# Attention and two expert stages: setup pinned ahead, the written order kept to unit 23, one prefill piece and late scatters of empty rows in place of four pieces

## The chip, the cores and the metric

The kernel runs on one core of one Trainium2 chip. The metric is the device time of one launch in microseconds. The core has TensorE (PE, matmuls), VectorE (DVE), ScalarE (ACT), GpSimd (POOL) and SyncE (SP, which issues most of the DMAs); 16 DMA engines serve them.

## What is computed

A linear attention with a per-channel decay, then two mixture-of-experts layers with one expert for each token. All in float32.

```python
# attention: B, H, S, D = 4, 8, 768, 48
f = 1 / (1 + exp(-f_logit))
for t in range(S):
    state = f[:, :, t, :, None] * state + einsum('bhd,bhe->bhde', k[:, :, t], v[:, :, t])
    y[:, :, t] = einsum('bhd,bhde->bhe', q[:, :, t], state)
x = y as [3072 tokens, 384]
# MoE 1: 8 experts, 384 -> 1024 -> 384
logits = normalize(x) @ normalize(emb).T / tau; e = argmax(logits); gate = softmax(logits)[e]
x1 = gate * (relu(x @ w1[e]) @ w2[e])
# MoE 2: the same size, for tokens with x1 @ w_skip > 0 only; the others keep x1
e, gate from softmax(x1 @ w_gate)
out = x1 + gate * (relu(x1 @ u1[e]) @ u2[e])
```

## The kernel before

**Attention.** The work is cut in 24 units: unit u is the chunk u // 4 of 128 positions of the batch row u % 4, all eight heads. For each unit the kernel loads q, k and f in one tile (`qkf`, four buffers, `a_load`) and v, takes exp and a running product of the decays (`gexp`, `scan`, `lnexp`, `nrm`), scales k and q with it (`khat`, `qp`, `qhat`), forms the masked scores (`score`, `amask`), multiplies with V and the state (`av`, copied out by `ytc`), updates the state (`kv`, `sup`; not for the last chunk, units 20 to 23), and projects to rows and router logits (`xout`, `xrow`, `xlg`). The work of several units overlaps. Which step of which unit comes in which iteration i (from -1 to 24) is written out by hand in the string STEADY, and in a second string from iteration 20 on; "khat+2" means khat of unit i + 2. Iteration i holds the score of unit i + 1. `ch` calls `pin`, which chains an instruction behind the last pinned one on its engine, so that the scheduler keeps the written order; before, it does so only up to iteration 20. What isn't pinned, the scheduler places by itself.

**Routing.** When four units of a chunk are done, `a_route` finds for each token the expert and its slot in the table `tab1` (448 ranks of 8 experts, rank-major, rows of 396 words), in ten small steps that letters R and Q in the order release; four indirect DMAs of POOL (`tab<-rows`, line 666) scatter the 128 rows each, at the letters S and T. Rows of the table that no token fills have to hold empty rows: `prefill` writes them beforehand from the tile `pf`, 512 rows at a time, from rank R0 = 192 on, in four pieces after the iterations 0, 1, 3 and 4. `tab2`, the table of the second layer, gets its seven pieces in iterations 15 to 19 and in block 0 of the experts.

**Between the stages.** After iteration 18 `star(0)` picks the expert with the most tokens so far (the star), and `w_load` loads its weights on SP; SP has to read the expert's number first. In iterations from 21 on the letter W lets `w_split` split pieces of its w1 in a high (ACT) and a low part (DVE). After iteration 21 `fill` raises the star's count to at least 318, the second half of the weights is loaded, and `x_load` reads the first 318 rows of the star from the table.

**Experts.** `experts` runs over blocks: block 0 is rows 0 to 317 of the star, block 1 the rest of the star up to 446 (it has at most 128 rows and goes through `flip1`), blocks 2 to 8 the other seven experts in falling order of their counts, each with a capacity out of CAPS1; then the same for the second layer. Steps f = 0 to 7 are the eight slices of the first product. In block 0 the last route's steps and its four scatters come after f = 0, `order(0)` after f = 2 (it sorts the experts and sets a flag when a count is over its capacity), and `x_load` of block 1 at f = 3. In block 1, at f = 3, `x_load` and `w_load` of block 2 follow each other on SP.

The setup is in two functions, `setup0` before the first unit, and `setup` (index tiles, the triangular matrix `lst`) at iteration 1, neither of them pinned:

```python
                if i == 1:
                    self.setup(st)
```

## Time and profile before

| | us |
|---|---|
| median of 3 runs | 591.59 (588.57 to 593.02) |
| the profiled execution | 590.0 |
| its span, first to last instruction | 588.3 |

Engines by busy share of the span: PE 95%, DVE 66%, ACT 55%, POOL 40%; mean granted clock of PE 0.979 of full speed. The DMA engines moved 101 MB. Times in the profile count from the span's start. A line of the profile's timeline has the start, the length, the engine with the line of the code, the operation, output <- input, shape, how often, and in brackets how long the engine had been idle before and what released it. In-order engines run their queue as it stands: an operation that waits holds all that is behind it.

### The profile page before, as it was taken

The page shows a single profiled execution, that of the slowest core. Times are in us where ns is not written, and L with a number is a line of the kernel's source. Part 1 is how long each engine was busy: PE and PEld are TensorE (multiplying, and loading weights), DVE is VectorE, ACT ScalarE, POOL GpSimd, SP SyncE. Part 2 cuts the span into 40 slices and gives each one's busy share as a digit, 9 for nine tenths or more (in the row PEclk, how much of TensorE's full clock was granted, in tenths as well). Part 3 has the DMA queues.
Part 4 walks back from the last instruction along what each step waited for, and adds up shares of the span by engine and source line. Part 5 has one row for each costly group of instructions (what it writes and reads, how often), then busy time and mean ns, then how long its engine had stood idle before and what let it go on. Part 6 is the DMA issues. An engine that isn't in the chain of part 4 may idle for free.

```text
span 588.3 us, 12419 instructions
## 1 busy us (share of the span) xinstructions
PE 557.7 (95%) x4549; PEld 528.5 (90%) x4551; DVE 389.0 (66%) x1125; ACT 323.7 (55%) x813; POOL 233.3 (40%) x231
## 2 busy tenths in 40 slices
PE   8699999988899999999999999999899999999992
PEld 4598999876799999999999999999799999999991
DVE  6699999997556857674878678856276637565000
ACT  7587777744536755565665555545165545544220
POOL 5577898785202500505076507442320203122111
PEclk9799999988999999999999999999899999999997
DMA  8999999967296542617082708630737077574700
GB/s 220 240 263 240 192 201 237 222 193 223 77 286 212 120 181 59 245 32 267 14 266 35 286 9 268 178 130 12 218 111 250 28 261 231 185 222 147 275 21 19
DMA packets 60367, 101.14 MB, mean 172 GB/s; under 512 B 16953, under 2 KB 48205, under 8 KB 60298
## 3 DMA queue, kind: packets, MB, share of 16 engines
q1 hardware_dynamic: 42138, 87.28, 50.1%
q0 software_dynamic: 17600, 12.95, 8.3%
q8 instruction: 38, 0.62, 0.5%
q14 instruction: 31, 0.25, 0.2%
q10 hardware_dynamic: 560, 0.03, 0.1%
HBM read 78.49 MB, written 27.17 MB: 180 GB/s over the span
## 4 chain that ended last, share of the span: by engine, by line
PE 64%; DVE 12%; issue 8%; DMA 8%; ACT 3%; POOL 3%; SPq 0%; POOLq 0%; DVEq 0%; ACTq 0%
PE ph L811 23%; PE pyt L811 22%; DMA xg<-tab 3%; DMA qkf<-qkf 2%; PE pxt L801 2%; PE pa L554 2%; PE py L576 2%; DVE at L561 2%; DVE qh L528 2%; PE px L611 2%; PE pyf L874 2%; PE py L573 2%; DVE ip L493 1%; PE py L924 1%; POOL out L976 1%
## 5 line engine op out<-in xcount | busy, mean ns | idle before, releaser
L811 PE MATMUL ph<-xh,w1h 128*128 128x318 f32 (+13 forms) x336 | 112.6, 336 | 1.2 <-ACT xh L805 0.8
L811 PE MATMUL pyt<-hh,w2h 128*128 128x318 f32 (+13 forms) x336 | 112.0, 333 | 0.4 <-ACT w2h L755 0.4
L811 PE MATMUL pyt<-hh,w2l 128*128 128x318 f32 (+13 forms) x336 | 109.6, 326 | 0.5 <-DVE w2l L756 0.5
L811 PE MATMUL pyt<-hl,w2h 128*128 128x318 f32 (+13 forms) x336 | 109.2, 325 | 0.0
L811 PE MATMUL ph<-xl,w1h 128*128 128x318 f32 (+13 forms) x336 | 109.2, 325 | 0.0
L811 PE MATMUL ph<-xh,w1l 128*128 128x318 f32 (+13 forms) x336 | 108.9, 324 | 0.0
L955 POOL DMA_INDIRECT tab<-x,idx x30 | 43.0, 1433 | 151.6 <-DVE idx L950 55.5
L845 DVE SCALAR_TENSOR_TENSOR hl<-ph,hh 128x318 fp32r<-128x318 f32 (+13 forms) x112 | 58.2, 520 | 41.0 <-ACT hh L844 40.3
L844 ACT ACTIVATE hh<-ph 128x318 fp32r<-128x318 f32 (+13 forms) x112 | 52.1, 465 | 49.4 <-PE ph L811 45.3
L756 DVE TENSOR_TENSOR w2l<-w2r,w2h 128x384 fp32r<-128x384 f32 x112 | 58.2, 549 | 17.1 <-ACT w2h L755 16.9
L811 PEld LDWEIGHTS ph<-xh,w1h 128*128 128x128 f32 x336 | 63.2, 188 | 2.1 <-ACT xh L805 1.2
L811 PEld LDWEIGHTS pyt<-hh,w2l 128*128 128x128 f32 x336 | 63.6, 189 | 1.4 <-DVE w2l L756 1.1
L811 PEld LDWEIGHTS pyt<-hh,w2h 128*128 128x128 f32 x336 | 63.8, 190 | 1.1 <-ACT w2h L755 0.6
L755 ACT CAST w2h<-w2r 128x384 fp32r<-128x384 f32 x112 | 51.7, 515 | 23.7 <-PE pyt L811 14.8
L811 PEld LDWEIGHTS pyt<-hl,w2h 128*128 128x128 f32 x336 | 63.9, 190 | 0.4 <-DVE hl L845 0.2
L811 PEld LDWEIGHTS ph<-xl,w1h 128*128 128x128 f32 x336 | 63.4, 189 | 0.2
L811 PEld LDWEIGHTS ph<-xh,w1l 128*128 128x128 f32 x336 | 63.2, 188 | 0.3
L756 DVE TENSOR_TENSOR w1l<-w1r,w1h 128x384 fp32r<-128x384 f32 x112 | 55.9, 558 | 7.6 <-ACT w1h L755 7.6
L976 POOL DMA_INDIRECT out<-yo,xg x17 | 19.2, 1129 | 94.8 <-DVE yo L974 92.9
L755 ACT CAST w1h<-w1r 128x384 fp32r<-128x384 f32 x112 | 49.0, 516 | 9.1 <-DMA w1r<-u 5.3
L960 POOL DMA_INDIRECT out<-x,oix x30 | 46.1, 1537 | 9.1 <-issue 9.1
L806 DVE TENSOR_TENSOR xl<-pxt,xh 128x128 fp32r<-128x128 f32 (+14 forms) x48 | 22.7, 490 | 29.3 <-ACT xh L805 22.8
(238 smaller groups left out, 1097.1 us busy)
## 6 DMA issues: line engine op xcount, KB each, us to landing
w1r<-w SPq DMA_DIRECT2D x8, 1536.0 KB
w2r<-w SPq DMA_DIRECT2D x8, 1536.0 KB
w1r<-u SPq DMA_DIRECT2D x8, 1536.0 KB
w2r<-u SPq DMA_DIRECT2D x8, 1536.0 KB
qkf<-qkf SPq DMA_DIRECT2D x40, 288.0 KB
tab<-pf SPq DMA_DIRECT2D x7, 776.0 KB
v<-v SPq DMA_DIRECT2D x24, 200.0 KB
xg<-tab SPq DMA_DIRECT2D x6, 594.0 KB
```

The source lines that it names most:

```text
L528: ch(nc.vector.scalar_tensor_tensor(out=w["qh"][:, s], in0=nr[:, s], scalar=2.0, in1=w["qp"][:, s], op0=ALU.subtract, op1=ALU.mult))
L554: ch(nc.tensor.matmul(w["pa"][k][:, p * C:(p + 1) * C], w["kh"][r:r + 64, p, :], w["qh"][r:r + 64, p, :], start=True, stop=True))
L561: ch(nc.vector.tensor_tensor(out=w["at"][:, k], in0=w["pa"][k].rearrange("q (p t) -> q p t", p=NP), in1=self.mask.unsqueeze(1).to_broadcas ...
L755: pin(nc.scalar.copy(hi[s], raw[s]))
L756: pin(nc.vector.tensor_tensor(out=lo[s], in0=raw[s], in1=hi[s].bitcast(F32), op=ALU.subtract))
L806: nc.vector.tensor_tensor(out=w["xl"][:, k, :N], in0=pt[:, :N], in1=w["xh"][:, k, :N].bitcast(F32), op=ALU.subtract)
L811: self.nc.tensor.matmul(out, l, r, start=(i == 0), stop=(i == n - 1))
L844: nc.scalar.activation(out=w["hh"][:, f, :N], in_=ph[:, :N], func=AF.Relu)
L845: nc.vector.scalar_tensor_tensor(out=w["hl"][:, f, :N], in0=ph[:, :N], scalar=0.0, in1=w["hh"][:, f, :N].bitcast(F32), op0=ALU.max, op1=AL ...
L955: last = nc.gpsimd.indirect_dma_start(out=self.v2[w["v0"] + j][:, :], out_offset=bass.IndirectOffsetOnAxis(ap=idx[:, j:j + 1], axis=0), in ...
L960: nc.gpsimd.indirect_dma_start(out=self.vo[w["v0"] + j][:, :], out_offset=bass.IndirectOffsetOnAxis(ap=oix[:, j:j + 1], axis=0), in_=xr[:T ...
L976: nc.gpsimd.indirect_dma_start(out=self.vo[w["v0"] + j][:, :], out_offset=bass.IndirectOffsetOnAxis(ap=w["xg"][:T, j, 386:387].bitcast(U32 ...
```

## The change

It does the following.

- `setup0` now holds nearly all of the setup, each instruction pinned, with the index tiles at the front of POOL's and DVE's queues; the constant part of `r1` is built there too. `setup` keeps a few memsets and is called at once.
- `ch` pins up to iteration 24, so the order of all units, with the W pieces and the scatters, stays as written.
- `a_load` issues f first and then q and k, as separate DMAs.
- `star` and `fill` work on the count in PSUM (`count`) with their small tiles beside it there, and have one or two operations less.
- R0 is 256. One prefill piece (ranks 256 to 319) after iteration 2 replaces the four. Ranks above come from `pads` and `pad`: after the last route's scatters in block 0, `pads` works out, for each expert, the 128 rows behind its last token; `pad(0)` scatters empty rows for the star, before `x_load` of block 1, and after that load `pad(1)` to `pad(8)` scatter them for the eight experts (the star's own indices among them are out of bounds). `order(0)` now flags a capacity that reaches more than 128 beyond the count, too.

```diff
-R0 = 192
+R0 = 256
...
-        self.v1 = dram_disjoint_views(self.tab1, NU)
+        self.v1 = dram_disjoint_views(self.tab1, NU + 9)
...
-    def setup0(self):
-        nc, cp, a = self.nc, self.cp, self.a
+    def setup0(self, su):
+        nc, cp, a, pin = self.nc, self.cp, self.a, self.pin
+        it = su.tile([128, 8], I32, name="it")
+        pin(nc.gpsimd.iota(it, pattern=[[1, 8]], base=0, channel_multiplier=0))
+        itk = su.tile([128, NCH, B], I32, name="itk")
+        pin(nc.gpsimd.iota(itk, pattern=[[C, NCH], [S, B]], base=0, channel_multiplier=1))
+        itp = su.tile([128, 1], I32, name="itp")
+        pin(nc.gpsimd.iota(itp, pattern=[[1, 1]], base=0, channel_multiplier=NE))
+        lf = su.tile([128, 128], F32, name="lf")
+        pin(nc.gpsimd.memset(lf, 1.0))
+        pin(nc.gpsimd.affine_select(out=lf, in_=lf, compare_op=ALU.is_gt, fill=0.0,
+                                    base=0, pattern=[[1, 128]], channel_multiplier=-1))
+        self.ef = cp.tile([128, 8], F32, name="ef")
+        pin(nc.vector.tensor_copy(self.ef, it))
+        self.wdesc = cp.tile([128, 8], F32, name="wdesc")
+        pin(nc.vector.tensor_scalar(out=self.wdesc, in0=self.ef, scalar1=-1.0, scalar2=8.0, op0=ALU.mult, op1=ALU.add))
+        pin(nc.vector.tensor_copy(self.pwd, self.wdesc))
+        self.tok = cp.tile([128, NCH, B], F32, name="tok")
+        pin(nc.vector.tensor_copy(self.tok, itk))
+        self.tku = cp.tile([128, NCH, B], U32, name="tku")
+        pin(nc.vector.tensor_copy(self.tku, self.tok))
+        self.p8 = cp.tile([128, 1], F32, name="p8")
+        pin(nc.vector.tensor_copy(self.p8, itp))
+        self.lst = cp.tile([128, 128], BF16, name="lst")
+        pin(nc.vector.tensor_copy(self.lst, lf))
+
...
-        make_identity(nc, self.ident)
+        pin(nc.gpsimd.memset(self.ident, 0.0))
+        pin(nc.gpsimd.affine_select(out=self.ident, in_=self.ident, compare_op=ALU.not_equal, fill=1.0,
+                                    base=0, pattern=[[-1, 128]], channel_multiplier=1))
+        pin(nc.gpsimd.memset(self.qkf[3][:, 2], 30.0))
...
+        pin(nc.gpsimd.memset(self.qkf[2][:, 0:2], 0.0))
+        pin(nc.gpsimd.memset(self.qkf[3][:, 0:2], 0.0))
+        self.r1 = su.tile([128, NP, 104], F32, name="r1")
+        for k in range(2):
+            pin(nc.gpsimd.tensor_copy(self.r1[:, :, 48 * k:48 * k + 48], self.ident[:, 64 * k:64 * k + 48].unsqueeze(1).to_broadcast([128, NP, 48])))
...
+        pin(nc.gpsimd.memset(pf, 0.0))
+        pin(nc.gpsimd.memset(pf[:, 385:386], OOB))
+        pin(nc.gpsimd.tensor_copy(pf[:, 386:387].bitcast(U32), pf[:, 385:386]))
...
-    def setup(self, su):
-        nc, cp, a = self.nc, self.cp, self.a
-        lf = su.tile([128, 128], F32, name="lf")
-        nc.gpsimd.memset(lf, 1.0)
-        nc.gpsimd.affine_select(out=lf, in_=lf, compare_op=ALU.is_gt, fill=0.0,
-                                base=0, pattern=[[1, 128]], channel_multiplier=-1)
-        self.lst = cp.tile([128, 128], BF16, name="lst")
-        nc.vector.tensor_copy(self.lst, lf)
+    def setup(self):
...
-        it = su.tile([128, 8], I32, name="it")
-        nc.gpsimd.iota(it, pattern=[[1, 8]], base=0, channel_multiplier=0)
-        ef = cp.tile([128, 8], F32, name="ef")
-        nc.vector.tensor_copy(ef, it)
-        self.ef = ef
-        self.wdesc = cp.tile([128, 8], F32, name="wdesc")
-        nc.vector.tensor_scalar(out=self.wdesc, in0=ef, scalar1=-1.0, scalar2=8.0, op0=ALU.mult, op1=ALU.add)
-        nc.vector.tensor_copy(self.pwd, self.wdesc)
-        itk = su.tile([128, NCH, B], I32, name="itk")
-        nc.gpsimd.iota(itk, pattern=[[C, NCH], [S, B]], base=0, channel_multiplier=1)
-        self.tok = cp.tile([128, NCH, B], F32, name="tok")
-        nc.vector.tensor_copy(self.tok, itk)
-        self.tku = cp.tile([128, NCH, B], U32, name="tku")
-        nc.vector.tensor_copy(self.tku, self.tok)
...
-        return ins if self.it > 20 else self.pin(ins)
+        return ins if self.it > NU else self.pin(ins)
...
-            for k in (2, 3):
-                nc.gpsimd.memset(self.qkf[k][:, 2], 30.0)
+            self.pin(nc.gpsimd.memset(self.qkf[2][:, 2], 30.0))
             self.setup_load(st)
-            self.setup0()
-            for k in (2, 3):
-                nc.gpsimd.memset(self.qkf[k][:, 0:2], 0.0)
+            self.setup0(st)
+            self.setup()
...
-                if i == 1:
-                    self.setup(st)
...
-                if i in (0, 1, 3, 4):
-                    self.prefill(self.tab1, R0 * NE // 512 + (0, 1, 3, 4).index(i))
+                if i == 2:
+                    self.prefill(self.tab1, R0 * NE // 512)
                 if i == NU - 2 * B + 2:
                     self.star(0)
                     self.w_load(w0)
...
-    def a_load(self, w, parts=(slice(0, 3), "v")):
+    def a_load(self, w, parts=(2, slice(0, 2), "v")):
...
     def star(self, m):
         nc, cp = self.nc, self.cp
         oh = self.star_oh[m]
-        c = self.total(self.acc[m], 8)
-        key = cp.tile([128, 8], F32, name="st_key%d" % m)
-        nc.vector.scalar_tensor_tensor(out=key, in0=c, scalar=8.0, in1=self.wdesc, op0=ALU.mult, op1=ALU.add)
+        pc = self.count(self.acc[m])
+        key, t, f = pc[:, 16:24], pc[:, 24:32], pc[:, 32:33]
+        nc.vector.scalar_tensor_tensor(out=key, in0=pc[:, 0:8], scalar=8.0, in1=self.wdesc, op0=ALU.mult, op1=ALU.add)
         mx = cp.tile([128, 1], F32, name="st_mx%d" % m)
         nc.vector.tensor_reduce(out=mx, in_=key, op=ALU.max, axis=AX.X)
         nc.vector.tensor_scalar(out=oh, in0=key, scalar1=mx, scalar2=None, op0=ALU.is_ge)
-        t = cp.tile([128, 8], F32, name="st_t%d" % m)
-        nc.vector.tensor_tensor(out=t, in0=oh, in1=self.ef, op=ALU.mult)
-        f = cp.tile([128, 1], F32, name="st_f%d" % m)
+        nc.vector.scalar_tensor_tensor(out=t, in0=key, scalar=mx[:, 0:1], in1=self.ef, op0=ALU.is_ge, op1=ALU.mult)
         nc.vector.tensor_reduce(out=f, in_=t, op=ALU.add, axis=AX.X)
         nc.vector.tensor_copy(self.sel[m][:, 0:1], f)
-        return c
-
-    def fill(self, m, c=None):
-        nc, cp = self.nc, self.cp
-        if c is None:
-            c = self.total(self.acc[m], 8)
+        return pc
+
+    def fill(self, m, pc=None):
+        nc = self.nc
+        if pc is None:
+            pc = self.count(self.acc[m])
+        c, d = pc[:, 0:8], pc[:, 40:48]
         if m == 0:
             nc.vector.tensor_scalar(out=self.ok[:, 16:24], in0=c, scalar1=float(R0), scalar2=None, op0=ALU.is_ge)
-        d = cp.tile([128, 8], F32, name="st_d%d" % m)
-        nc.vector.scalar_tensor_tensor(out=d, in0=c, scalar=float(NA[m]), in1=c, op0=ALU.max, op1=ALU.subtract)
-        nc.vector.tensor_tensor(out=d, in0=d, in1=self.star_oh[m], op=ALU.mult)
+        nc.vector.tensor_scalar(out=d, in0=c, scalar1=-1.0, scalar2=float(NA[m]), op0=ALU.mult, op1=ALU.add)
+        nc.vector.scalar_tensor_tensor(out=d, in0=d, scalar=0.0, in1=self.star_oh[m], op0=ALU.max, op1=ALU.mult)
         nc.vector.scalar_tensor_tensor(out=self.acc[m], in0=d, scalar=self.ident[:, 0:1], in1=self.acc[m],
                                        op0=ALU.mult, op1=ALU.add)
+
+    def count(self, acc):
+        pc = self.ps("r", "pc")
+        self.nc.tensor.matmul(pc[:, :8], self.onesf, acc, start=True, stop=True)
+        return pc
+
+    def pads(self):
+        nc, sm = self.nc, self.sm
+        c = self.total(self.acc[0], 8)
+        base = sm.tile([128, 8], F32, tag="p_b", name="p_b")
+        nc.vector.scalar_tensor_tensor(out=base, in0=c, scalar=float(NE), in1=self.ef, op0=ALU.mult, op1=ALU.add)
+        nc.vector.tensor_scalar(out=base, in0=base, scalar1=self.p8[:, 0:1], scalar2=None, op0=ALU.add)
+        t = sm.tile([128, 8], F32, tag="p_t", name="p_t")
+        nc.vector.tensor_tensor(out=t, in0=base, in1=self.star_oh[0], op=ALU.mult)
+        s = sm.tile([128, 1], F32, tag="p_s", name="p_s")
+        nc.vector.tensor_reduce(out=s, in_=t, op=ALU.add, axis=AX.X)
+        self.padi = self.cp.tile([128, 9], U32, name="padi")
+        nc.vector.tensor_copy(self.padi[:, 0:1], s)
+        nc.vector.scalar_tensor_tensor(out=self.padi[:, 1:9], in0=self.star_oh[0], scalar=OOB, in1=base, op0=ALU.mult, op1=ALU.add)
+
+    def pad(self, j):
+        self.nc.gpsimd.indirect_dma_start(
+            out=self.v1[NU + j][:, :], out_offset=bass.IndirectOffsetOnAxis(ap=self.padi[:, j:j + 1], axis=0),
+            in_=self.pf, in_offset=None, bounds_check=NE * STRIDES[0] - 1, oob_is_err=False)
 
...
-        nc.vector.tensor_tensor(out=self.ok[:, 8 * m:8 * m + 8], in0=sc, in1=self.caps[:, m, :], op=ALU.is_le)
+        le = self.ok[:, 8 * m:8 * m + 8]
+        nc.vector.tensor_tensor(out=le, in0=sc, in1=self.caps[:, m, :], op=ALU.is_le)
+        if m == 0:
+            nc.vector.scalar_tensor_tensor(out=key, in0=sc, scalar=128.0, in1=self.caps[:, m, :], op0=ALU.add, op1=ALU.is_ge)
+            nc.vector.tensor_tensor(out=le, in0=le, in1=key, op=ALU.mult)
...
                     self.steps(-1)
                     while self.pend:
                         self.pend.pop(0)()
+                    self.pads()
+                    self.pad(0)
...
                         self.x_load(n)
                     if n["new"]:
                         self.w_load(n)
+                    if i == 0:
+                        for j in range(8):
+                            self.pad(1 + j)
```

## Rows read from the trace of the kernel before

**Rows 1.** The page, busy us of each engine (share of the span) and instructions.

```profile
PE 557.7 (95%) x4549; PEld 528.5 (90%) x4551; DVE 389.0 (66%) x1125; ACT 323.7 (55%) x813; POOL 233.3 (40%) x231
```

**Rows 2.** Stretches: length; busy PE, PEld, DVE, ACT, POOL (instructions); clock, DMA share, GB/s.

```profile
20.00:25.00 5.00, 5.00 (x49) 4.07 (x51) 2.07 (x6) 3.14 (x7) 3.16 (x3) 0.61 1.03 226
25.00:55.00 30.00, 28.80 (x425) 25.97 (x424) 28.09 (x65) 23.06 (x51) 19.87 (x20) 1.00 1.02 263
...
165.00:185.00 20.00, 19.54 (x128) 17.49 (x127) 8.52 (x44) 8.76 (x24) 0.19 (x1) 1.00 1.03 333
```

**Rows 3.** Timeline of PE, units 0, 1 and 7 (py: V product, pa: score).

```profile
19.31 0.69 PE L576 MATMUL py<-at,v 128*64 128x128 f32 x2 [5.12 <-DVE at L561]
...
24.28 1.16 PE L554 MATMUL pa<-qh,kh 64*128 64x128 f32 x16
...
54.01 1.16 PE L554 MATMUL pa<-qh,kh 64*128 64x128 f32 x16 [1.09 <-DVE npl L531]
```

**Rows 4.** Timeline of DVE, up to the first mask multiply.

```profile
4.49 0.69 DVE L493 TENSOR_TENSOR_SCAN ip<-e,lim 128x258 f32<-128x258 f32 x1 [2.42 <-ACT e L485]
...
16.39 0.17 DVE L138 CAST ef<-it 128x8 f32<-128x8 int32 x1 [1.98 <-POOL it L136]
...
17.98 0.68 DVE L514 TENSOR_TENSOR kh<-qkf,ip 128x512 f32<-128x512 f32 x1
18.58 1.27 DVE L561 TENSOR_TENSOR at<-pa,mask 128x512 f32<-128x512 f32 x2
```

**Rows 5.** Timeline of ACT, the exp of unit 4.

```profile
21.12 0.63 ACT L484 ACTIVATE e<-qkf 128x512 f32<-128x512 f32 x1 [4.28 <-DMA qkf<-qkf]
```

**Rows 6.** Timeline of PE, unit 19 to blocks 0 and 2.

```profile
115.76 1.16 PE L554 MATMUL pa<-qh,kh 64*128 64x128 f32 x16
...
119.11 0.41 PE L653 MATMUL pr<-acc,onesf 128*128 128x32 f32 x2 [1.87 <-DVE tot L987]
...
124.50 1.16 PE L554 MATMUL pa<-qh,kh 64*128 64x128 f32 x16
...
128.71 1.16 PE L554 MATMUL pa<-qh,kh 64*128 64x128 f32 x16
...
143.90 0.93 PE L554 MATMUL pa<-qh,kh 64*128 64x128 f32 x6
...
151.44 0.55 PE L811 MATMUL ph<-xh,w1h 128*128 128x318 f32 x2 [0.85 <-ACT xh L805]
...
188.93 0.36 PE L811 MATMUL ph<-xh,w1h 128*128 128x432 f32 x1
```

**Rows 7.** Timeline of SP and ACT, the star's w1: issue and first split.

```profile
124.66 0.43 SPq L736 DMA_DIRECT2D w1r<-w  x1
...
132.30 0.51 ACT L755 CAST w1h<-w1r 128x384 fp32r<-128x384 f32 x1 [1.50 <-DMA w1r<-w]
```

**Rows 8.** Timeline of DVE, a route operation and the star's key.

```profile
109.18 0.19 DVE L658 SCALAR_TENSOR_TENSOR pr<-pr,ef 128x32 f32<-128x32 f32 x1
...
119.57 2.17 DVE L679 SCALAR_TENSOR_TENSOR st_key<-tot,wdesc 128x8 f32<-128x8 f32 x1
```

**Rows 9.** Timeline of SP, loads of blocks 1 and 2.

```profile
161.99 0.38 SPq L771 DMA_DIRECT2D xg<-tab  x1
...
169.59 2.20 SPq L771 DMA_DIRECT2D xg<-tab  x2
173.76 0.40 SPq L736 DMA_DIRECT2D w1r<-w  x1
```

**Rows 10.** Timeline of ACT, block 1's tokens and block 2's first splits.

```profile
165.61 0.52 ACT L779 ACTIVATE sq<-xg 128x384 f32<-128x384 f32 x1 [2.93 <-DMA xg<-tab]
...
187.03 1.34 ACT L755 CAST w1h<-w1r 128x384 fp32r<-128x384 f32 x3
```

**Rows 11.** Timeline of POOL, scatters of the last route and of block 0.

```profile
159.16 0.98 POOL L666 DMA_INDIRECT tab<-rows,idx  x1 [0.30 <-issue]
...
188.68 1.95 POOL L955 DMA_INDIRECT tab<-x,idx  x1 [0.30 <-ACT w1h L755]
```

More of the change, by code (lines that the diff above doesn't have):

```diff
@@ L110, in setup0 @@
-        nc.gpsimd.affine_select(out=self.mask, in_=self.mask, compare_op=ALU.is_ge, fill=0.0,
-                                base=0, pattern=[[1, 128]], channel_multiplier=-1)
+        pin(nc.gpsimd.memset(self.mask, -1.0))
+        pin(nc.gpsimd.affine_select(out=self.mask, in_=self.mask, compare_op=ALU.is_ge, fill=0.0,
+                                    base=0, pattern=[[1, 128]], channel_multiplier=-1))
+        pin(nc.gpsimd.memset(self.qkf[2][:, 0:2], 0.0))
+        pin(nc.gpsimd.memset(self.qkf[3][:, 0:2], 0.0))
@@ L179, in setup_r1 @@
         nc.vector.tensor_scalar(out=emb, in0=emb, scalar1=self.er[:, 0:1], scalar2=self.rtau[:8, 0:1], op0=ALU.mult, op1=ALU.mult)
-        self.r1 = su.tile([128, NP, 104], F32, name="r1")
         pe = self.ps("y", "pe")
@@ L184, in setup_r1 @@
         nc.vector.tensor_copy(self.r1[:, :, 96:104], pe[:, :32].rearrange("q (p e) -> q p e", p=NP))
-        for k in range(2):
-            nc.gpsimd.tensor_copy(self.r1[:, :, 48 * k:48 * k + 48], self.ident[:, 64 * k:64 * k + 48].unsqueeze(1).to_broadcast([128, NP, 48]))
     def setup_r2(self):
```

6 lines of the change are left out of this document (1 added, 5 removed).

## The prediction

> **What bounds the kernel now.** I read the busy table first: TensorE (PE) works 95% of the span [rows 1], so time can only come out of stretches where it waits or runs at half clock. The list of score matmuls shows where. From the score of unit 1 at 24.28 to that of unit 19 at 115.76 there are 18 units, 5.08 us each [rows 3, 6]: PE's own work with hardly a gap. What doesn't fit that pace lies at both ends of the attention stage.
>
> At the start PE stands for 5.12 us in front of the first product with V, waiting for the masked scores of unit 0, and unit 1's score comes only at 24.28 [rows 3]. The reader should follow that wait into VectorE (DVE): it is in order, and ahead of the mask multiply at 18.58 it had stood 1.98 us for an iota of `setup`, then ran five small setup operations up to 17.98 [rows 4]. The clock pays as well: after PE's gap the granted clock in 20 to 25 us is 0.61, against 1.00 in 25 to 55 us [rows 2]. And ScalarE (ACT) waits 4.28 us, up to 21.12, for unit 4's load of 576 KB (2 x 48 x 3 x 512 words) [rows 5], in a stretch where the DMA engines are busy all the time (share 1.03 and 1.02, 226 and 263 GB/s) [rows 2].
>
> At the end the pace breaks again: unit 19's score is at 115.76, unit 20's at 124.50, unit 21's at 128.71; the last piece of unit 23's is at 143.90, and the MoE begins at 151.44 [rows 6]. One cause is in the same rows: a matmul of the route (`pr`, line 653), which no chain pins after iteration 20, was put ahead of older work and held PE for 1.87 us until DVE had copied `tot` [rows 6].
>
> **Part 1, setup first, loads split, three prefill pieces gone.** Removed from DVE between 14.4 and 17.98: the wait and these five operations, 3.6 us from the end of the operation before (16.39 less the 1.98 idle = 14.41) to 17.98, when khat of unit 2 runs, with the mask behind it at 18.58 [rows 4]. They now stand ahead of the first scan, which starts at 4.49 after 2.42 us of idle time [rows 4]; that idle time hides them, and about the same work on GpSimd (POOL). Without that cover they would cost what they cost now. So the mask comes about 3.6 us earlier, PE's 5.12 us of waiting shrink to 1.5, and I expect the clock not to fall. What PE runs from 19.31 to 24.28 takes 4.97 us there, partly at 0.61 [rows 2, 3]; at full clock I estimate 3.5. Sum: 3.6 + 1.5 = 5.1 us earlier for unit 1.
>
> The gain holds only if ACT doesn't then stand in front of unit 4's load with unit 0's copy-out queued behind it [rows 5]. Here the split counts: `gexp` needs only the f third, now sent first. One third of 576 KB at the 226 GB/s of that stretch is 0.9 us against 2.6 [rows 2], so f lands some 1.7 us before the whole, about 19.4, and earlier yet by what is no longer in the queues. Later, three pieces of 811 KB (512 rows of 396 words) are gone, 2.4 MB or 9 us of a busy DMA at 263 GB/s [rows 2]. That buys only what still waits behind loads: unit 7's score starts 1.09 us late [rows 3]. I take all of it, so the start gives 5.1 + 1.1 = 6.2 us. Bounds: 2 if ACT's wait for unit 4 stays where it was, 7.5 if the whole 5.12 goes along with clock and the 1.1. The two more DMA issues for each unit sit on SyncE (SP), which has nothing else to do there: nothing.
>
> **Part 2, the order kept to the last unit.** At an undisturbed pace unit 20 comes 5.08 after unit 19. Units 20 to 23 have no state update and need less; 124.50 to 128.71 shows 4.21 [rows 6]. Unit 23's score would end at 115.76 + 5.08 + 3 x 4.21 + 1.16 (one score) = 134.6, against 143.90 + 0.93 = 144.8 now: 10.2 us to win at most. The price of pinning is that the splits of the first weight tile (`w_split`) are now in the chain too, three per iteration from 21 on. If w1 has not landed, ACT and DVE stand, with unit 21's copy-out behind the first two. Now w1's load is issued at 124.66, 8.9 us after unit 19's score, and is used at 132.30, 7.6 us later [rows 7]. In the issue lies the star chain on DVE: it includes a key operation of 2.17 us, while the route's operation of the same form on PSUM takes 0.19 [rows 8]; its first operand and its output are now in PSUM, and the copy is gone. I take 2.5 us off: issue at 6.4, landing at 14.0 after unit 19's score. Two splits and the copy-out, some 0.5 us each on ACT [rows 7], bring unit 21 on at 15.5. PE is ready for it at 5.08 + 2 x 4.21 + 1.16 = 14.7. So about 0.8 us of wait, 3.3 if the star chain gets no faster. With another 1.4 us for what I can't place (POOL's 1.3 us scatters in the same iterations) I take 10.2 - 2.2 = 8.0 us. Bounds: 4 and 10.2. The other chain, from the route's indices through four scatters to `x_load` of the first block, moves by a similar amount, since its steps are pinned in iterations 20 and 21.
>
> **Part 3, the late scatters.** Nine scatters of empty rows come after the last four of the route; one has only rows out of bounds. What is queued behind them counts: block 1's `x_load` is behind the first; the other eight write the table that this load reads, so I let them start when it has landed, and block 2's `x_load` waits for them, with block 2's w1 and w2 loads behind it on SP. Now: `x_load` of block 1 at 161.99, landed at 165.61; of block 2 at 169.59, its w1 at 173.76; the splits of w1 begin at 187.03, block 2's matmuls at 188.93 [rows 6, 9, 10]. After, in the same frame: seven small DVE steps among other work and one scatter put block 1's `x_load` about 2.3 us later (164.3), landed 167.9. Eight scatters of 0.98 + 0.30 us [rows 11] are 10.3 us, then the 1.85 us that lie between the end of the last scatter (160.14) and the load now [rows 9, 11]: block 2's `x_load` at about 180.9, 11.3 later. If w1 keeps its 4.2 us behind it, it is issued at 185.1 and lands 7.6 later at 192.7; the first split has at most 188.93 - 187.03 - 0.5 = 1.4 us to spare, so 4.3 us are lost, and I estimate 1.7 more when w2 lands behind it: 6. If the two weight loads go ahead of that `x_load`, only the tokens are late, by some 2 us (block 1's load took 3.6 us to land, so 184.5 or later, and the transposes come a few us ahead of 188.93). I take 4.0, the middle. Bounds: 0, if the eight start without waiting for block 1's load, and 19 (the last rival). The bytes are no matter by themselves: 1.6 MB at the 333 GB/s of 165 to 185 us is 4.9 us [rows 2], and that ends before w2 is needed.
>
> On the scatters a rule and the trace differ. In the trace the next scatter starts 1.28 us after the one before, and only the last is followed by about 1.85 us [rows 9, 11]. The Trainium skill ("DMA: Bandwidth & Descriptors", section "Anatomy of one DMA") gives each DMA of this path a fixed 2.0 us plus its bytes at 436 GB/s, by estimate 2.5 us for such a scatter; laid end to end eight would be 20 us in place of 10.3 and the sum 589.5. The rows show that they overlap, so I stay with them; slower scatters are the last rival, priced from rows.
>
> **The sum.** Against the profiled execution, 590.0 us (span 588.3 and 1.7 around it): 590.0 - 6.2 - 8.0 + 4.0 = 579.8. That execution lies 1.6 us under the median 591.59. I say 580.
>
> **Rivals.**
> *Weights late.* The star chain stays as slow, and pinned splits hold ACT and DVE for 3.3 us, with half clock behind it, so that the end gives 4 in place of 8: 584. For it: 8.9 us from score to issue [rows 6, 7]. Against: the 2.17 us operation loses its cause.
> *The start is the DMA's.* Its share is over 1.0 from 20 to 55 us [rows 2]; if unit 4's f lands no earlier, ACT's wait keeps unit 0's copy back and the start gives 2 in place of 6.2: 584. Against: after unit 1 PE keeps its pace although all four pieces are in flight.
> *Slower, through the scatters alone.* Scatters from the expert stage start 1.95 + 0.30 us apart [rows 11]. At that pace eight take 18.0 us, 7.7 more than I took, so with the weights behind them on SP the loss is 6 + 7.7 = 13.7. Such a gap lowers the clock (20 to 25 us at 0.61 lost 5 x 0.39 = 2 us [rows 2]), and block 1's tokens, for which ACT already waits 2.93 us with split work behind it [rows 10], are 2.3 + 1.0 later: 19.0 in all, or 594.8. It decides from the point at which block 2's weights come more than 14.2 us late, the gain of the two other parts. Against it: the scatter at 159.16 and its three neighbours, nearest in kind and time, keep 1.28 [rows 11].
>
> **How the numbers follow.** Likeliest case 0.55, own range 574 to 586; weights late 0.15; start unchanged 0.12; scatters slower 0.10; two of these at once, 588 to 596, 0.08. 573 to 589 holds the first three and leaves out less than 0.2. Faster by over 1% (about what a measurement can tell from no change here) means under 585.7: 0.51 of the first case and 0.17 of the next two, 0.68. Slower means over 597.5, which takes the scatter case or two cases at once at their far end: 0.08. The same: 0.24.
>
> **What would show it.** Right: unit 1's score near 19.2, unit 7's near 47.8 (now 54.01), clock 1.00 in 20 to 25 us; no `pr` matmul of the route ahead of its unit; MoE's first matmul near 137; block 2's first matmul 38 to 44 us after that (37.5 now) [rows 6]. Wrong: ACT idle before unit 4's exp; ACT's first w1 split with a long wait on the load inside iteration 21; eight scatters more than 1.5 us apart, or block 2's weights issued only after them and PE idle for over 8 us there.

## The result, and the profile after

The changed kernel takes 583.63 us (median; 581.71 to 585.2) against 590.91 (588.57 to 593.02) for the kernel before, timed beside it: ratio 0.9875, 95% interval 0.984 to 0.991, so 1.25% faster (0.9 to 1.6%). 580.0 was forecast, 573 to 589 as the range. Its profiled execution takes 582.3 (span 580.6, before 588.3): 7.7 us less, where the sum of the prediction had 10.2 less.

The timeline of TensorE (PE) in the kernel after shows the three stretches (start, length, engine and line, operation, how often, idle time before and its releaser). These rows answer to [rows 3, 6]; the last is block 2's first matmul.

```profile
12.86 2.08 PE L558 MATMUL pa<-qh,kh 64*128 64x128 f32 x16 [1.19 <-DVE qh L532]
21.90 1.16 PE L558 MATMUL pa<-qh,kh 64*128 64x128 f32 x16
50.47 1.16 PE L558 MATMUL pa<-qh,kh 64*128 64x128 f32 x16
...
111.79 1.16 PE L558 MATMUL pa<-qh,kh 64*128 64x128 f32 x16
116.67 1.16 PE L558 MATMUL pa<-qh,kh 64*128 64x128 f32 x16
121.38 1.16 PE L558 MATMUL pa<-qh,kh 64*128 64x128 f32 x16 [0.43 <-DVE lim L620]
126.94 1.16 PE L558 MATMUL pa<-qh,kh 64*128 64x128 f32 x16 [0.38 <-DVE qh L532]
131.93 1.16 PE L558 MATMUL pa<-qh,kh 64*128 64x128 f32 x16
...
140.37 1.12 PE L831 MATMUL pxt<-ident,xga 106*128 106x106 f32 x6 [2.18 <-DMA xga<-tab]
141.48 0.90 PE L841 MATMUL ph<-xh,w1h 128*128 128x318 f32 x2
...
181.43 0.36 PE L841 MATMUL ph<-xh,w1h 128*128 128x432 f32 x1
```

- Start: unit 1's score is 2.4 us earlier (24.28 before), unit 7's 3.5 (54.01), unit 19's 4.0 (115.76).
- End: from unit 19's score to the MoE's first matmul 29.69 us (141.48 - 111.79) against 35.68, a gain of 6.0.
- MoE: from its first matmul to block 2's 39.95 us (181.43 - 141.48) against 37.49: 2.5 given back.

4.0 + 6.0 - 2.5 = 7.5, nearly the whole 7.7.

The timeline of VectorE (DVE), to be read beside [rows 4], shows what the start lost.

```profile
5.62 0.16 DVE L177 RECIPROCAL rtau<-tau 128x1 f32<-128x1 f32 x1 [3.55 <-DMA tau<-tau]
5.71 0.12 DVE L214 TENSOR_SCALAR n_cl<-es 8x1 f32<-8x1 f32 x1
...
7.59 0.53 DVE L190 TENSOR_SCALAR emb<-emb,er,rtau 8x512 f32<-8x512 f32 x1
8.05 0.15 DVE L117 CAST ef<-it 128x8 f32<-128x8 int32 x1
...
8.88 0.21 DVE L128 CAST lst<-lf 128x128 bf16<-128x128 f32 x1
9.01 1.26 DVE L497 TENSOR_TENSOR_SCAN ip<-e,lim 128x258 f32<-128x258 f32 x2
```

The setup casts are where the change put them, ahead of the first scan. But the norm of the embedding (`setup_en`), which nothing pins, was placed ahead of them all, and its first step waits 3.55 us for the load of `tau`. The first scan starts at 9.01 instead of 4.49, so the scores of unit 0 come at 12.86 instead of 10.12.

Granted clock and DMA, by the table of stretches (PEclk, DMA share and GB/s are the last three columns), beside [rows 2]:

```profile
10.00:15.00 5.00, 3.07 (x21) 2.40 (x22) 4.88 (x14) 4.43 (x12) 0.51 (x1) 0.59 0.96 221
15.00:20.00 5.00, 5.00 (x26) 2.71 (x27) 3.77 (x6) 4.24 (x11) 4.67 (x4) 0.72 1.05 233
20.00:25.00 5.00, 5.00 (x63) 3.84 (x58) 3.63 (x8) 4.00 (x10) 3.95 (x4) 1.00 0.82 204
25.00:55.00 30.00, 29.95 (x450) 27.28 (x451) 28.98 (x69) 25.12 (x58) 23.15 (x23) 1.00 0.87 219
120.00:130.00 10.00, 8.99 (x120) 7.85 (x118) 9.64 (x28) 4.92 (x12) 8.82 (x11) 1.00 1.03 322
142.00:144.00 2.00, 2.00 (x10) 1.99 (x9) 1.31 (x6) 1.70 (x7) 0.00 (x0) 0.50 0.00 0
```

The low clock has moved forward, from 15 to 25 us (before 0.71 and 0.61) to 10 to 20 us (0.59 and 0.72), behind the wait above. In 25 to 55 us the DMAs have slack now (0.87, before 1.02). In 142 to 144 us, just after the MoE begins, the clock is 0.50, that is 1.2 of 2.4 GHz: PE had waited 2.18 us for the first gathered rows. Before, the half clock of this handover fell ahead of the MoE (0.50 in 140 to 142 us, the MoE at 151.44).

The late scatters, in the timelines of GpSimd (POOL), of SP's queue and of ScalarE (ACT), beside [rows 9, 10, 11]:

```profile
130.68 1.42 POOL L670 DMA_INDIRECT tab<-rows,idx  x1 [0.30 <-issue]
135.62 1.92 SPq L801 DMA_DIRECT2D xga<-tab  x2
...
153.80 0.37 SPq L801 DMA_DIRECT2D xg<-tab  x1
157.03 1.44 POOL L724 DMA_INDIRECT tab<-pf,padi  x1 [4.73 <-DMA xg<-tab]
...
166.57 0.98 POOL L724 DMA_INDIRECT tab<-pf,padi  x1 [0.30 <-issue]
170.10 1.87 SPq L801 DMA_DIRECT2D xg<-tab  x2
173.31 0.41 SPq L766 DMA_DIRECT2D w1r<-w  x1
180.06 1.34 ACT L785 CAST w1h<-w1r 128x384 fp32r<-128x384 f32 x3 [0.41 <-DMA w1r<-w]
```

The eight scatters do wait for block 1's load and end at 167.55; block 2's gather is issued 28.6 us after the MoE's first matmul (29.5 forecast) and w1 behind it. Yet ACT waits only 0.41 us for w1. Something else gave the 2.5 us back. The table of stretches, from the MoE's first matmul to block 2's, first before and then after (the second number is PE's busy time), splits the loss:

```profile
151.44:188.93 37.49, 36.64 (x242) 33.81 (x243) 22.20 (x99) 18.02 (x51) 5.93 (x7) 1.00 0.66 216
141.48:181.43 39.95, 37.77 (x244) 35.01 (x244) 22.79 (x106) 18.07 (x50) 15.32 (x16) 0.97 0.60 206
```

PE is busy 1.1 us longer, at a mean granted clock of 0.97 instead of 1.00, and idle 1.3 us longer (39.95 - 37.77 = 2.18 against 0.85).

### The profile page after: what moved, and what is told of

It reads as the page before. It is cut to its first block, busy times and chain, and to the rows that moved or that the text cites. A ratio compares the mean times of both kernels' runs of the same rounds, so it can differ in the third digit from the quotient of the medians.

```text
span 580.6 us, 12506 instructions
## 1 busy us (share of the span) xinstructions
PE 554.2 (95%) x4553; PEld 526.0 (91%) x4553; DVE 382.8 (66%) x1132; ACT 324.6 (56%) x813; POOL 246.5 (42%) x241
## 4 chain that ended last, share of the span: by engine, by line
PE 67%; issue 10%; DMA 10%; DVE 5%; POOL 3%; ACT 1%; SPq 1%; POOLq 0%; DVEq 0%; ACTq 0%
PE pyt L841 21%; PE ph L841 21%; PE pa L558 4%; PE py L580 3%; PE px L615 3%; PE py L577 3%; DMA tab<-x,idx 2%; PE pxt L831 2%; PE pt L544 2%; DMA w2r<-w 2%; DMA xg<-tab 2%; DMA w1r<-u 2%; PE pk L595 1%; POOL out L1006 1%; DVE w2l L786 1%
## 5 line engine op out<-in xcount | busy, mean ns | idle before, releaser
L786 DVE TENSOR_TENSOR w2l<-w2r,w2h 128x384 fp32r<-128x384 f32 x112 | 58.3, 550 | 19.7 <-ACT w2h L785 19.4
L1006 POOL DMA_INDIRECT out<-yo,xg x17 | 19.2, 1129 | 94.8 <-DVE yo L1004 93.0
L990 POOL DMA_INDIRECT out<-x,oix x30 | 48.0, 1601 | 9.1 <-issue 8.5
```

The source lines that it names most:

```text
L786: pin(nc.vector.tensor_tensor(out=lo[s], in0=raw[s], in1=hi[s].bitcast(F32), op=ALU.subtract))
L990: nc.gpsimd.indirect_dma_start(out=self.vo[w["v0"] + j][:, :], out_offset=bass.IndirectOffsetOnAxis(ap=oix[:, j:j + 1], axis=0), in_=xr[:T ...
L1006: nc.gpsimd.indirect_dma_start(out=self.vo[w["v0"] + j][:, :], out_offset=bass.IndirectOffsetOnAxis(ap=w["xg"][:T, j, 386:387].bitcast(U32 ...
```

## The experiments

All ratios are to the kernel before, timed beside the kernel in question on the same chip; the changed kernel's is 0.9875 (0.984 to 0.991). It was not timed beside the experiments (e1 to e4 stand together, e5 to e8, and e9 to e11), so small differences of ratios are to be read with their intervals. "M" is the MoE's first matmul. Marks are read from one profiled execution of each kernel. Where the code is the same, they still differ: unit 19's score stands at 111.75 to 112.95 in the changed kernel, e2, e4, e5 and e6, and at 108.78 to 111.00 in e1, e7, e9 and e11.

**e1: the norm kept behind unit 0's kh.**

```diff
-        nc.vector.reciprocal(out=self.rtau, in_=self.tau)
+        self.pin(nc.vector.reciprocal(out=self.rtau, in_=self.tau))
...
-        en = self.norm(es, 8, 1)
+        en = self.norm(es, 8, 1, self.pin)
...
-        nc.vector.tensor_scalar(out=cl, in0=ss, scalar1=2.0 ** -60, scalar2=None, op0=ALU.max)
+        pin(nc.vector.tensor_scalar(out=cl, in0=ss, scalar1=2.0 ** -60, scalar2=None, op0=ALU.max))
```

> The changed kernel, with two more pins: the embedding-norm steps that wait for the load of tau (the reciprocal of tau and the first step of the norm) stay behind unit 0's first kh on VectorE, so that the setup casts and unit 0's scans no longer stand behind that load. Theory (the missing 2.4 us of the start were lost in this one wait of 3.55 us and the seven steps behind it, 9.01 against 4.49 for the first scan): first scan at 4.5 to 5, unit 0's score at about 10.1 instead of 12.86, unit 1's at about 19.2 instead of 21.90, unit 7's at about 48 instead of 50.47, the first MoE matmul about 2.5 earlier (139.0 against 141.48), time 2 to 3 us below the changed kernel. Rival (the loads set the start): unit 0 and unit 1 move as above, but the wait of unit 4's e for its load grows from 1.44 to about 4 us, unit 7's score stays at 50 and later, and the time is within 1 us of the changed kernel.

Ratio 0.9878 (0.9825 to 0.9931): no faster than the changed kernel. PE's timeline:

```profile
10.10 1.16 PE L558 MATMUL pa<-qh,kh 64*128 64x128 f32 x16 [0.34 <-DVE qh L532]
17.77 1.16 PE L558 MATMUL pa<-qh,kh 64*128 64x128 f32 x16
48.63 1.16 PE L558 MATMUL pa<-qh,kh 64*128 64x128 f32 x16
...
130.87 1.16 PE L558 MATMUL pa<-qh,kh 64*128 64x128 f32 x16
140.14 1.32 PE L831 MATMUL pxt<-ident,xga 106*128 106x106 f32 x6 [3.11 <-DMA xga<-tab]
141.44 0.90 PE L841 MATMUL ph<-xh,w1h 128*128 128x318 f32 x2
177.02 0.95 PE L831 MATMUL pxt<-ident,xg 108*128 108x108 f32 x4 [3.33 <-DMA xg<-tab]
```

The cause of the start's loss holds: units 0, 1 and 7 come 2.8, 4.1 and 1.8 us earlier than in the changed kernel. (Unit 1 at 17.77 is the earliest of five kernels with this start; e7, e8, e9 and e11 have 18.32 to 21.19. Unit 7 is at 47.45 to 49.67 in the five, against 49.81 to 51.11 where the norm stands in front.) But unit 23 is only 1.1 earlier, and M not at all: PE waits 3.11 us for the first gather instead of 2.18. And block 2's gather, which the changed kernel just met, is now 3.33 us late, and half clock follows it (PEclk is the third number from the end):

```profile
176.00:178.00 2.00, 0.98 (x5) 1.01 (x6) 0.00 (x0) 0.00 (x0) 0.00 (x0) 0.66 0.97 346
178.00:180.00 2.00, 2.00 (x9) 1.89 (x9) 1.43 (x11) 0.52 (x1) 0.00 (x0) 0.50 0.99 399
```

So the time is within 1 us of the changed kernel's, as the rival had it, but not for its reason: unit 4's load holds ACT for 2.00 us and not 4, unit 7 does come earlier, and two gathers behind the start take the gain.

**e2: block 2's w1 ahead of its `x_load`.**

```diff
+                    if i == 1:
+                        self.w_load(n)
                     if "xg" not in n:
                         self.x_load(n)
-                    if n["new"]:
+                    if n["new"] and i != 1:
                         self.w_load(n)
```

> The changed kernel, but block 2's w1 is issued on SP ahead of block 2's x_load instead of behind it, so that it doesn't stand behind the nine late scatters. Theory (the MoE's give-back of 2.3 us is that w1 comes late, which delays the first w1h split and the work of ScalarE and VectorE between the blocks): w1 is issued about 12 us after the first block's scatters instead of 32 us after the first MoE matmul (before: 22), the first w1h split stands at 36 us or less after the first MoE matmul (38.6 now), block 2's first matmul at 37.5 to 38 after it (39.95 now), time about 2 us below the changed kernel. Rival 1 (the scatters' own traffic, or the gather of block 2 behind them, delays block 2): block 2's first matmul stays at 39.9 after the first. Rival 2: w1's 1.5 MB now collides with the scatters, x_load of block 2 lands later, and block 2 starts later than 40 after the first.

Ratio 0.9988 (0.9963 to 1.0014): the whole gain is lost. w1 is issued at 161.18, and the gather of block 2 slips to 174.99, 32.4 us after M: 6.7 us behind the end of the last scatter (168.26), in the changed kernel 2.5 (170.10 - 167.55).

```profile
161.18 0.41 SPq L766 DMA_DIRECT2D w1r<-w  x1
174.99 1.89 SPq L801 DMA_DIRECT2D xg<-tab  x2
180.82 0.98 PE L831 MATMUL pxt<-ident,xg 108*128 108x108 f32 x4 [6.51 <-DMA xg<-tab]
```

Block 2 starts 46.8 us after M. Rival 2 holds. That w1 was late finds no support: with w1 12 us earlier block 2 starts later. What matters behind the scatters is the gather.

**e3: four prefill pieces again, no late scatters.** (`R0 = 192`, the pieces after units 0, 1, 3, 4, `pads` and `pad` gone.)

> The changed kernel with its third part undone: four prefill pieces after units 0, 1, 3 and 4 (R0 = 192), and neither pads nor late scatters; the setup and the order of the end stay changed. Theory (the pieces cost the start what the scatters cost the MoE's first block): block 2's first matmul goes back to 37.5 us after the first MoE matmul (39.95 now), a gain of 2.4; DMA share of 25 to 55 us goes back above 1.0 from 0.87 and unit 7's score waits again, later by about 1 us (51.5 against 50.47); the time is 0 to 2 us below the changed kernel, so that this part as made is a loss. Rival (the freed DMA time carried most of the start's 3.5 us): unit 7's score at 53 or later, time 1 to 2 us above the changed kernel.

Ratio 0.9928 (0.9894 to 0.9963), 0.5% above the changed kernel, with overlapping intervals. Unit 7's score is at 50.56, as in the changed kernel, unit 19's at 113.88, 2.1 later; the end takes 33.4 us instead of 29.7 (w1 is issued 7.6 us after unit 19 instead of 5.5). Block 2 starts 39.82 us after M although no late scatter stands in front of it. But this handover is worse: PE waits 4.0 us for the first gather, runs at 0.50 until 3.5 us after M, and waits 1.6 us for a split of w2. So the run neither clears the scatters nor measures what the pieces cost; e6 and e10 say more.

**e4: the order free again from iteration 21.** (`self.it > 20` in `ch`.)

> The changed kernel with the limit of the written order put back (free from iteration 21 on); all else stays changed. Theory (of the 10 us by which the MoE starts earlier, about 4 are the start's and 6 are the kept order of the end): unit 19's score as in the changed kernel (111.8), first MoE matmul at 147.5 (141.48 now; 151.44 before), time 5 to 6 us above the changed kernel. Rival (the quicker star alone, 2.0 us less at its key and w1 issued 3.4 us earlier after unit 19, makes the end shorter, and the order does little): first MoE matmul at 144 or earlier, time at most 3 us above.

Ratio 0.9939 (0.9909 to 0.9968). From unit 19's score (112.47) to M (145.32) 32.85 us, between the kernel before (35.68) and the changed one (29.69): the kept order is worth 3.2 us of the end's 6.0; the other 2.8 are left, by subtraction, for the quicker star and what goes with it. M lies between the two expectations (147.5, and 144 or earlier), and so does the time by the ratios, 3.8 us more; the medians (585.44 against 583.63) have 1.8.

**e5: w2 of the first expert issued behind the first `x_load`.** (`w0["load2"]()` moved behind `self.x_load(w0)`.)

> The changed kernel, but the load of w2 for the first expert (1.5 MB) is issued on SP behind the first x_load instead of 17 us ahead of it. Theory (the end is bounded by the bulk in the DMA queues: w1, a piece of tab2 and w2, 3.8 MB issued at 117.3 to 118.6 and moved at 310 to 400 GB/s until about 134, behind which the last scatter's packets land 3.5 us after it instead of 1.9, so that the three matmul-side microseconds that the pinned norm won in the first experiment were all given back at this gather): last scatter to x_load's issue about 2 us instead of 3.5, x_load to its landing 4 to 5 us, first MoE matmul at about 139 instead of 141.48, the wait of TensorE for xga below 1 us. Rival (the scatters' own chain from the routing index sets it, whatever else is in the queues): x_load is issued at 135 to 136 as before, first MoE matmul at 141 to 142. Rival 2: w2 comes late and the first block waits for it: first MoE matmul earlier, but its hl or w2l steps wait.

Ratio 0.9989 (0.9967 to 1.0011), but for a reason that none of the three named. `x_load` follows the last scatter's end by 2.24 us (136.06 - 133.82) instead of 3.52 (135.62 - 132.10), as the theory has it. With the new order the scheduler put the first block's transposes ahead of unit 23's `px` on PE:

```profile
141.54 0.86 PE L831 MATMUL pxt<-ident,xga 106*128 106x106 f32 x6 [3.61 <-DMA xga<-tab]
142.20 1.91 PE L615 MATMUL px<-r,yt 128*128 128x104 f32 x8
```

`px` stands 5 us later than in the changed kernel (137.06), and with it the last routing, the scatters and block 2's gather, for which PE then waits 5.74 us. The run doesn't decide its question for M; e7 and e9 do.

**e6: the last routing ahead of the first block.** The five steps, the scatters, the pads' index and the first pad stand ahead of block 0's transposes, `x_gate` behind them; the five steps, the transposes with their copies and the first operations of `x_gate` are pinned (not shown below).

```diff
-            self.it = 99
             self.rg.append([self.a_route(NCH - 1), "v"])
-            for _ in range(4):
-                self.steps(1)
+            self.steps(-1)
+            self.it = 99
+            while self.pend:
+                self.pend.pop(0)()
+            self.pads()
+            self.pad(0)
...
-        self.x_T(W[0], (0, 1, 2))
+        self.x_T(W[0], (0, 1, 2), self.pin)
```

> The changed kernel, but the last chunk's routing (its five steps on VectorE, its matmuls, its four scatters, the padding index and the first pad) stands ahead of the first block's transposes on TensorE and VectorE, instead of among its first matmuls, and x_gate behind them. Theory (in the MoE the late scatters delay block 2's gather itself, not w1: it lands just when TensorE needs it in the changed kernel and 3.3 us late in the first experiment): the scatters start at about 141 to 142 instead of 146.17, pad 0 at 147 instead of 151.3, x_load of block 2 at about 166 instead of 170.1 (24.5 after the first MoE matmul instead of 28.6), no wait of TensorE for block 2's rows, block 2's first matmul at 37.5 to 38.5 after the first MoE matmul (39.95 now), time about 1.5 to 2 us below the changed kernel. Rival (what is late is the split of w1, by ScalarE's and VectorE's own work): x_load of block 2 comes 4 us earlier, and block 2's first matmul stays at 39.5 to 40 after the first.

Ratio 0.981 (0.9766 to 0.9854), 0.65% or some 3.8 us below the changed kernel, with intervals that just overlap; of this the marks show 1.2 us (block 2's first matmul at 180.27 against 181.43). The scatters start at 142.43, block 2's gather is issued at 167.01, 24.3 us after M (142.76), PE doesn't wait for it, and block 2 starts 37.51 us after M, as expected. That is the 37.49 of the kernel before, with all nine late scatters in place.

**e7: e1, e5 and e6 together; e8: that, and tab2's pieces in iterations 13, 15 and 17.**

> The first, the fifth and the sixth experiment in one kernel: the norm pinned in its place, w2 behind the first gather, the last routing ahead of the first block. Theory (start, end and first blocks each have one bound, and each edit moves its own, so that the gains add): unit 0's score at 10.1, unit 23's at 130.9 or earlier, first MoE matmul at about 138, block 2's first matmul 37.5 to 38.5 after it, time 576 to 579. Rival (the bounds hand the gain on to the next wait, as in the first experiment): the marks at the front move, but the time stays within 1 us of the changed kernel's 583.

> As the seventh, and the three prefill pieces of tab2 two iterations earlier (13, 15, 17 instead of 15, 17, 19), so that none is issued between w1 and the last gather. If the queues' bulk still sets the first gather in the seventh kernel, the first MoE matmul comes another 0.5 to 1.5 us earlier; if not, within 0.3 us of the seventh and the same time.

e7: ratio 0.9776 (0.9735 to 0.9817), 577.35 us. Unit 23's score is at 130.24, M at 139.42 (9.18 us later; forecast 138), block 2 38.02 after M. The gains add where each gather has room. e8: ratio 0.9801 (0.9768 to 0.9833); unit 23 and M are both 0.43 us earlier than in e7, 9.18 apart again, so that piece of tab2 delays nothing. Block 2's gather has little room even so: in e8 PE waits 1.03 us for it.

**e9: e7 without the move of w2.**

> The seventh kernel without its move of w2: the norm pinned and the last routing ahead, w2 issued where the changed kernel has it. Theory (the 1.5 MB of w2 in the queues delay the first gather by 1 to 2 us): time from unit 23's score to the first MoE matmul 10 to 10.6 us as in the first experiment, instead of 9.18 in the seventh; first MoE matmul 1 to 1.5 us later than in the seventh for the same unit 23, time 1 to 1.5 us above the seventh (ratio to the kernel before about 0.980 against 0.9776). Rival (the scatters' chain alone sets the gather): the same 9.2 us and the same time as the seventh.

Ratio 0.983 (0.9803 to 0.9857). From unit 23's score (128.34) to M (138.51) 10.17 us, 1.0 more than in e7 and e8. The first gather is issued 3.78 us behind the end of the last scatter (132.65 - 128.87) instead of 2.23 in e7 (132.99 - 130.76): w2 in the queues costs it 1.5 us. M gets 1.0 of that, since in e7 PE waits for the last routing (1.77 us) and not for the gather. The intervals of the times overlap, so only the marks show it.

**e10: e7 with the four pieces in place of the pads.**

> The seventh kernel with the third part of the change undone (four prefill pieces at the start, no pads, no late scatters). Theory (the pieces hold up the loads of the first units, the late scatters cost little once they are started early): unit 19's score 2 us later than the seventh's 110.67, no scatters between the first and the third block, block 2's first matmul 37 to 38 us after the first MoE matmul as in the seventh (38.02), time 2 to 3 us above the seventh. Rival (late scatters still cost the MoE 1 to 2 us, as forecast): block 2's first matmul at 36 to 36.5 after the first MoE matmul, time equal to the seventh's or below it.

Ratio 0.9858 (0.9837 to 0.9878), 0.8% above e7; against e9, timed beside it, 0.3%, with overlapping intervals. Unit 19's score comes at 113.80 instead of 110.67, 3.1 us later (2.8 to 5.0 against e7, e9 and e11), lost between unit 7 (49.68) and unit 10 (67.56): 17.9 us, in e7 15.4; block 2 starts 36.88 after M, against 38.02 in e7 and 36.58 in e9. The pieces cost the attention stage some 3 us, and leaving out scatters that start early enough wins the MoE at most 1.1 us: by the marks replacing the pieces was a gain.

**e11: e7 with eight matmuls of zeros while PE waits at the handover.**

```diff
+            pz = self.ps("tr", "pz")
+            for _ in range(8):
+                self.ch(nc.tensor.matmul(pz, self.z[:, 0:128], self.z, start=True, stop=True))
             self.rg.append([self.a_route(NCH - 1), "v"])
```

> The seventh kernel with eight matmuls of zeros (128x512 bf16, into a bank that nothing reads) on TensorE behind unit 23's px, where it waits 1.8 us for the last routing and then for the first rows. Theory (the 2.5 us by which block 2 stands later after the first MoE matmul than in the kernel before are mostly the granted clock, 0.50 for the first 2.5 to 6 us of the MoE after TensorE's idle time, and neither the scatters nor w1): granted clock 1.00 in 140 to 146, first pyt 12.4 us after the first MoE matmul instead of 14.42 in the seventh, block 2's first matmul about 36 after it instead of 38.02, time 1.5 to 2 us below the seventh. Rival (the half clock stands beside waits that hide it): the clock rises, block 2's first matmul stays at 37.5 to 38, the time stays.

The stretch of 142 to 144 us in the table of stretches, in e7 (PEclk is the third number from the end):

```profile
142.00:144.00 2.00, 2.00 (x9) 2.00 (x9) 1.15 (x7) 1.62 (x7) 1.55 (x2) 0.50 0.51 197
```

and in e11:

```profile
142.00:144.00 2.00, 2.00 (x15) 1.92 (x15) 1.31 (x8) 2.00 (x9) 1.70 (x2) 1.00 0.52 198
```

The clock stays at 1.00, and block 2 starts 36.62 us after M instead of 38.02: 1.4 us. Ratio 0.979 (0.9769 to 0.9811), 576.03 us; e9, timed beside it, has 0.983 (0.9803 to 0.9857), and e7, timed earlier, 0.9776. So the mark moved forward by most of what was expected (36), and in the time it can't be told from e7.

One more row limits what this shows. e9 has no zeros, and its clock is 0.50 for only 3.4 us after M (138.51), half as long as in e7 (6.5):

```profile
142.00:144.00 2.00, 2.00 (x15) 2.00 (x15) 1.01 (x5) 1.78 (x8) 1.39 (x3) 1.00 0.31 118
```

Its block 2 starts 36.58 us after M, as early as with the zeros. In e11 PE gets to its first `pyt` sooner and waits there:

```profile
152.69 0.41 PE L848 MATMUL pyt<-hh,w2h 128*128 128x318 f32 x1 [0.84 <-DVE hl L882]
```

In e9 nothing waits there. So in these kernels some 3 us of half clock behind M cost the mark nothing, because DVE's `hl` would have held PE about as long; the 1.4 us are the price of the longer stretch in e7. e7 and e11 are the fastest: some 1% below the changed kernel, 2.1 to 2.2% below the kernel before.

The marks of PE side by side, in us after M (worked out from each kernel's timeline):

| kernel | first `pyt` of block 0 | block 1's transposes | block 2's first matmul | last two apart |
|---|---|---|---|---|
| before | 12.39 | 20.92 | 37.49 | 16.57 |
| after | 14.25 | 22.67 | 39.95 | 17.28 |
| e1 | 14.27 | 21.33 | 44.16 | 22.83 |
| e2 | 13.80 | 20.87 | 46.76 | 25.89 |
| e3 | 13.62 | 23.24 | 39.82 | 16.58 |
| e4 | 12.48 | 21.15 | 39.61 | 18.46 |
| e5 | 13.79 | 20.83 | 44.90 | 24.07 |
| e6 | 13.93 | 20.94 | 37.51 | 16.57 |
| e7 | 14.42 | 21.45 | 38.02 | 16.57 |
| e8 | 13.05 | 20.07 | 37.63 | 17.56 |
| e9 | 12.97 | 20.00 | 36.58 | 16.58 |
| e10 | 13.29 | 20.32 | 36.88 | 16.56 |
| e11 | 12.90 | 20.02 | 36.62 | 16.60 |

16.57 or so is the least from block 1's transposes to block 2, with PE busy throughout. e1, e2, e4, e5 and e8 lie above it, by 1.0 to 9.3 us; those are the kernels in which PE waits for block 2's gather (3.33, 6.51, 1.95, 5.74 and 1.03). Where the wait is over 3 us (e1, e2, e5), another 1.8 to 2.9 us are lost behind it, at half clock (shown above for e1); in e4 and e8 the clock stays at 1.00 and nothing more is lost. The changed kernel lies 0.7 above it with no wait for the gather: PE's weight loads of block 1 wait 0.6 us for ACT's `xh` and 0.4 for DVE's `xl`. The larger part of its 2.5 us, 1.75, is there before block 1's transposes.

## Why the prediction was right, and where its steps failed

The total holds (583.63 in 573 to 589, faster by over 1%) because all three terms came out at some 0.6 to 0.75 of their size, the gains and the loss alike: 4.2 us of gain are missing, and 1.5 us of loss. That these partly cancel is luck, since the loss came about in another way than forecast.

**Part 1 (forecast 6.2, measured 3.5 at unit 7, 4.0 at unit 19).** The failed step is "that idle time hides them": I looked at the casts that the change pins and not at what stays free beside them. The norm, whose wait for `tau` had stood behind the first scan, was put in front of both. e1 shows it: with the norm in its place unit 0's score is at 10.10 and unit 1's at 17.77 (19.2 forecast). It shows as well that the rival (the start is the DMA's) was half right: of the 4.1 us that unit 1 wins there, 1.8 are left at unit 7, with ACT waiting 2.00 us for unit 4's load. In the changed kernel too ACT waits 1.44 us there, one of my signs of being wrong, and unit 4's exp starts at 20.77 (f forecast at 19.4; before 21.12). With the norm in place unit 7 comes 5.4 us earlier than before in e1, and 4.3 to 6.6 in the five kernels with that start, around the 6.2. What I expected of the clock in 20 to 25 us came true (1.00). The split of the loads was undone in no run, so its share is not shown.

**Part 2 (forecast 8.0, measured 6.0).** The mechanism holds: units 20 to 23 keep their pace (4.88, 4.71, 5.56 and 4.99 us apart), no `pr` stands ahead of its unit, the star's key takes 0.17 instead of 2.17 us, w1 is issued 5.5 us after unit 19 (6.4 forecast), and ACT waits 0.96 for it. Up to the end of unit 23's score the gain is 7.8 us (21.30 after unit 19's score against 29.07), close to the 8.0; 1.8 are lost between there and M (8.39 against 6.61). What failed is the step that I passed over with "moves by a similar amount", the route's own chain. PE waits 2.18 us for the first gather: its last scatter ends at 132.10, the load is issued 3.5 us later and lands 4.75 after that, while w1, a piece of tab2 and w2 fill the queues (share 1.03, 322 GB/s). With w2 behind the gather (e7 against e9) M comes 1 us sooner after unit 23; what holds the rest of the chain was not tried.

**Part 3 (forecast a loss of 4.0, measured 2.5).** The sizes of the queue were right (block 1's load 12.3 us after M, 12.9 forecast; block 2's gather 28.6, 29.5 forecast; scatters 1.28 us apart). The 29.5 has a slip in it: 167.9 + 10.3 + 1.85 is 180.05 and not 180.9, so the working gives 28.6, just what was measured, and a loss of some 3.5 in place of 4.0. The step that failed is the victim: "its w1 ... lands", then 4.3 us lost and 1.7 more. w1 came 0.41 us late, and e2 shows that it is the wrong thing to hurry. What the trace shows in its place is half clock behind PE's wait at the handover, 0.50 until 2.6 us after M (PE busy 1.1 us longer), and steps of ACT and DVE that come late in blocks 0 and 1 (PE idle 1.3 us longer):

```profile
154.31 0.42 PE L841 MATMUL ph<-xh,w1h 128*128 128x318 f32 x1 [0.56 <-DVE hl L875]
...
158.20 0.41 PE L841 MATMUL pyt<-hh,w2l 128*128 128x318 f32 x1 [1.06 <-DVE w2l L786]
```

Before, PE waits there 0.38 us for `w2h` and not for `hl`; a first wait for `hl` of 0.4 both kernels have. PE's weight loads of block 1 wait 1.0 for `xh` and `xl` together. e6, which takes the last routing out of DVE's work in block 0, leaves PE without a wait behind M and brings back 2.4 us in spite of a longer half clock (0.50 from 142 to 148 us). So the late steps are shown by experiment. For the half clock there is only the sum above: no run takes it alone out of the changed kernel, and e9 against e11 shows that as much of it (there with the last routing ahead) can cost nothing. I had the half clock at the start and in a rival, not at the handover.

**The rivals.** Weights late: no (0.96 us). Slower scatters: no. The Trainium skill's rule that I weighed ("DMA: Bandwidth & Descriptors", section "Anatomy of one DMA") would have had eight in some 20 us by estimate; the trace has 10.5 (157.03 to 167.55), so its fixed 2 us are not paid one after the other. But the danger behind that rival is real: block 2's gather had no slack, and a kernel that reaches it 2 us sooner (e1) or delays it (e2) waits for it over 3 us and then runs at half clock.

## What to carry to other kernels

When a change pins one group of instructions, list what stays free on the same engine and what it waits for: the scheduler may put exactly that in front. A stage that starts earlier only helps if the gathers behind it have slack; ask for each transfer when it could land, not only which of them is issued last. An engine's wait at a handover can cost a second time when the clock falls behind it; whether it does, only the marks further on tell.
